# Four DMA transposes per batch queued later, and the last block sums put behind their products, in a fused attention and MLP kernel

## The chip, the cores and the metric

The kernel runs on one core of a Trainium2 chip. The metric is device time in microseconds (us) of one execution. Executions of one kernel agree within about 0.3%. Engines are called PE (TensorE matmul), PEld (TensorE weight load), DVE (VectorE), ACT (ScalarE), POOL (GpSimd) and SP (SyncE, which here only issues DMAs).

## The reference

```python
# u, v: [8, 3008, 256], z: [8, 3008, 64], float32
scores = (z @ z^T) / 3008
attn   = maximum(scores, 0) ** 2
x      = u * (attn @ v)                    # reshaped to [24064, 256]
h      = x @ w_in                          # [24064, 2048]
out    = (h * sigmoid(1.702 * h)) @ w_out  # [24064, 256]
```

The score matrix is symmetric, and the kernel uses that: it computes about half of the blocks and gets the other half by transposing on the DMA engines.

## The kernel before

A batch has 24 blocks of 128 rows in 6 chunks of 512 columns (chunk 5 is short). A *unit* (i, jp) is a pair of row blocks against chunk i: two PE matmuls, a Relu on ScalarE, a square on VectorE into a tile `a`. Where the mirrored block is needed, SyncE issues a DMA transpose of `a` into a tile `tt`. All transposes of a batch go through SyncE's one queue, in program order.

```python
def square(b, i, jp, sc):
    rl = pw.tile([P, 2, CH], F16, name="rl", tag="rl", bufs=3)
    ...
    act.activation(rl, sc, AF.Relu, scale=csc)
    ...                                   # diagonal units: a small transpose into "ad"
    a = pa.tile([P, 2, CH], F16, name="a", tag="a", bufs=21)
    unit[b, i, jp] = a
    dve.tensor_tensor(a, rl, rl, ALU.mult)
    cj = jp // 2
    if cj > i and (b or cj < NCH - 1):
        if (b, i, cj) not in TT:
            TT[b, i, cj] = pa.tile([P, CB, CB, P], F16, name="tt", tag="tt", bufs=14)
        k0 = 2 * (jp % 2)
        sp.dma_start_transpose(
            TT[b, i, cj][:, k0:k0 + 2].rearrange("p r g c -> p (r g) c"),
            a.rearrange("p r c -> p (r c)"),
        )
```

The order of the units puts the last chunk's (10 and 11) ahead of units 6 to 9. Chunk 0 has units 0..5, 10, 11, 6..9, chunk 1 has 2..5, 10, 11, 6..9, and so on:

```python
def pieces(b, i):
    lst = [(i, jp) for jp in range(2 * i if b or i < NCH - 1 else 0, NU)]
    if i == NCH - 1 or b == 0:
        return lst
    k = max(len(lst) - 6, 2)
    return lst[:k] + lst[-2:] + lst[k:-2]
```

Attention of chunk i multiplies the blocks of v with the scores. Each block is used twice (for two halves of the output), and a chunk takes about 11 to 13 us. The blocks j = 20, 21, 22 come last in the first half; for them PE reads the transposes of units (i, 10) and (i, 11), so these are *chunk i's last-chunk tiles*. The transposes of (0, 6) to (0, 9) are read only in the attention of chunks 3 and 4.

Chunk 0's units are computed at the end of the batch before, those of chunks 1 and 2 during attention of chunks 0 and 1.

The MLP's second product is done by a Strassen scheme: seven products P1 to P7 per chunk on PE, with block sums (S1 to S4, two halves each) on VectorE:

```python
prods = products(nst(b))
for q in range(head, nup):
    ...
    up_group(b, q)               # each up group also pops one waiting sum
    product(b, *prods.pop(0))
for kp in prods:                 # only the last batch has any left: 14
    for s_ in SUMS[:2]:
        s_()
    del SUMS[:2]
    product(b, *kp)
```

```python
# in product():
if name in ("P1", "P6", "P7"):
    u_ = ST[b, k, "after" + name] = pw.tile([P, 2, P], F32, name="u" + name, tag="u" + name, bufs=1)
    act.activation(u_, bank, AF.Copy, scale=1.0 / FSC)
...
outs = {"P2": (0, C0, "P2", "P1"), "P7": (1, C1, "P5", "P7"), "P3": (0, C1, "P5", "P6")}
if name in outs:
    o, c, x, u_ = outs[name]
    dve.scalar_tensor_tensor(     # "y"
        y[:, :, o, c], ST[b, k, "bank" + x], 1.0 / FSC, ST[b, k, "after" + u_], ALU.mult, ALU.add,
    )
```

P6, P7 and P4 accumulate onto P1's bank, P3 onto P5's. So a product may have to wait until ScalarE has copied its bank into a `uP` buffer, and each of these buffers exists once: it is free when the `y` of the block before has read it.

## Time and profile before

| | before |
|---|---|
| median time, range (3 runs) | 1206.41 us, 1205.06 to 1208.82 |
| profiled span | 1203.2 us, clock 1.000 |
| PE busy | 1190.2 us |
| PE's waits in all | about 9 us, 6 of them in the start-up |

The page of the kernel before: busy time and share of the span of each engine, TensorE's granted clock in 40 slices, and the chain of waits by engine.

```profile
PE 1190.2 (99%) x11785; PEld 715.2 (59%) x11785; DVE 830.5 (69%) x1277; ACT 770.5 (64%) x903; POOL 307.1 (26%) x363
...
PEclk9999999999999999999999999999999999999999
...
PE 95%; DMA 2%; DVE 2%; ACT 1%; issue 0%; SPq 0%; ACTq 0%; DVEq 0%
```

PE is the limit everywhere. So the change can only win what PE waits. PE's table of waits in the kernel before (engine and line that waited, what for, us in total, times, longest):

```profile
PE o L304 <- DMA tt<-a: 2.0, 5, 0.7
...
PE st L445 <- ACT uP L455: 0.9, 1, 0.9
```

The first line is attention waiting for transposed tiles, the second one product waiting for ScalarE. The change aims at both. Its first target, in SyncE's timeline of batch 2 (start, length, engine, line, operation, count):

```profile
305.06 19.15 SPq L251 DMA_TRANSPOSE tt<-a  x10
324.63 1.19 SPq L238 DMA_TRANSPOSE ad<-a  x1
325.92 11.77 SPq L251 DMA_TRANSPOSE tt<-a  x8
337.80 2.33 SPq L238 DMA_TRANSPOSE ad<-a  x1
```

And PE in the same stretch:

```profile
332.71 0.83 PE L304 MATMUL o<-tt,V 64*128 64x512 f16 x6
334.28 1.04 PE L304 MATMUL o<-tt,V 64*128 64x512 f16 x8 [0.74 <-DMA tt<-a]
```

The group of 10 is chunk 0 (units 2..5, 10, 11, then 6..9); the group of 8 is chunk 1, whose fourth transpose is unit (1, 11). SyncE's queue runs back to back here: an issue takes 1.28 us in the median of all transposes and the next one begins 0.1 us later, so a place in the queue costs about 1.38 us (these 8 took 11.8 us, as the first needed 2.1). PE's matmul at 334.28 us is the first that needs (1, 11). It waited 0.74 us.

The second target is at the kernel's end. These lines of the timeline of the kernel before are VectorE's, ScalarE's and PE's around the wait:

```profile
1186.66 1.95 PE L445 MATMUL st<-WT,s 128*128 128x128 f16 x32
...
1187.40 1.29 DVE L416 TENSOR_TENSOR s<-gt 128x1024 f16<-128x1024 f16 x2
...
1188.61 0.42 DVE L461 SCALAR_TENSOR_TENSOR y<-st,uP 128x256 f32<-128x256 f32 x1
...
1189.12 0.38 ACT L455 ACTIVATE uP<-st 128x256 f32<-128x256 f32 x1 [2.69 <-DVE y L461]
1189.55 1.05 PE L445 MATMUL st<-WT,gt 128*128 128x128 f16 x16 [0.94 <-ACT uP L455]
```

Read upwards: PE's P7 waits for ScalarE's copy, that for VectorE's y, and y stood behind two sums.

### The profile page before, as it was taken

The page shows a single profiled execution, that of the slowest core. Times are in us where ns is not written, and L with a number is a line of the kernel's source. Part 1 is how long each engine was busy: PE and PEld are TensorE (multiplying, and loading weights), DVE is VectorE, ACT ScalarE, POOL GpSimd, SP SyncE. Part 2 cuts the span into 40 slices and gives each one's busy share as a digit, 9 for nine tenths or more (in the row PEclk, how much of TensorE's full clock was granted, in tenths as well). Part 3 has the DMA queues.
Part 4 walks back from the last instruction along what each step waited for, and adds up shares of the span by engine and source line. Part 5 has one row for each costly group of instructions (what it writes and reads, how often), then busy time and mean ns, then how long its engine had stood idle before and what let it go on. Part 6 is the DMA issues. An engine that isn't in the chain of part 4 may idle for free.

```text
span 1203.2 us, 28259 instructions
## 1 busy us (share of the span) xinstructions
PE 1190.2 (99%) x11785; PEld 715.2 (59%) x11785; DVE 830.5 (69%) x1277; ACT 770.5 (64%) x903; POOL 307.1 (26%) x363
## 2 busy tenths in 40 slices
PE   7999999999999999999999999999999999999998
PEld 2446765467644676446765468554775547844577
DVE  7669954597545976469654696648966489564886
ACT  6777684476844768366683666736677376772764
POOL 4144300352004520044200451015510134101000
PEclk9999999999999999999999999999999999999999
DMA  9966399562994639844399454984459754496012
GB/s 225 169 112 129 114 168 158 86 153 72 169 161 89 151 91 174 159 78 137 94 186 146 80 137 98 194 133 76 138 121 183 133 83 149 114 180 117 1 37 71
DMA packets 366592, 152.33 MB, mean 127 GB/s; under 512 B 313312, under 2 KB 358496, under 8 KB 366464
## 3 DMA queue, kind: packets, MB, share of 16 engines
q1 hardware_dynamic: 330320, 114.08, 48.6%
q0 software_dynamic: 35456, 35.86, 14.8%
q8 instruction: 92, 1.51, 0.5%
q10 hardware_dynamic: 688, 0.59, 0.2%
q14 instruction: 36, 0.29, 0.1%
HBM read 60.29 MB, written 24.64 MB: 71 GB/s over the span
## 4 chain that ended last, share of the span: by engine, by line
PE 95%; DMA 2%; DVE 2%; ACT 1%; issue 0%; SPq 0%; ACTq 0%; DVEq 0%
PE o L304 37%; PE hg L345 26%; PE st L445 17%; PE yp L511 8%; PE sc L217 6%; DMA tt<-a 2%; DVE a L245 1%; ACT rl L231 0%; DMA zf<-in_z_dram 0%; DVE gt L354 0%; DVE zst L123 0%; ACT gf L353 0%; DVE s L416 0%; DVE s L418 0%; PE zp L129 0%
## 5 line engine op out<-in xcount | busy, mean ns | idle before, releaser
L353 ACT ACTIVATE gf<-hg 128x1024 f32<-128x1024 f32 (+1 forms) x384 | 385.8, 1007 | 166.0 <-PE hg L345 138.8
L231 ACT ACTIVATE rl<-sc 128x1024 f16<-128x1024 f32 x311 | 308.1, 1025 | 208.0 <-PE sc L217 205.9
L304 PEld LDWEIGHTS <-V 64*128 64x128 f16 (+1 forms) x4052 | 233.9, 94 | 251.4 <-issue 10.0
L345 PE MATMUL hg<-xt,W 128*128 128x512 f16 (+1 forms) x1408 | 354.5, 374 | 0.1
L354 DVE TENSOR_SCALAR gt<-gf 128x1024 f16<-128x1024 f32 (+1 forms) x384 | 275.5, 718 | 89.0 <-ACT gf L353 84.7
L245 DVE TENSOR_TENSOR a<-rl 128x1024 f16<-128x1024 f16 x276 | 192.0, 697 | 183.8 <-ACT rl L231 181.0
L304 PE MATMUL o<-a,V 64*128 64x512 f16 (+2 forms) x2010 | 316.4, 372 | 0.0
L187 POOL DMA_DIRECT2D uq<-in_u_dram x188 | 129.6, 696 | 509.2 <-PE sc L217 343.5
L304 PE MATMUL o<-tt,V 64*128 64x512 f16 (+1 forms) x1762 | 215.3, 376 | 2.0 <-DMA tt<-a 2.0
L345 PEld LDWEIGHTS <-W 128*128 128x128 f16 x1536 | 141.2, 98 | 117.5 <-issue 0.3
L445 PEld LDWEIGHTS <-gt 128*128 128x128 f16 x2176 | 132.5, 98 | 29.8 <-issue 1.1
L217 PE MATMUL sc<-ZT 64*128 64x512 f16 (+1 forms) x692 | 121.3, 366 | 1.9 <-ACT ZT L135 0.9
L445 PEld LDWEIGHTS <-s 128*128 128x128 f16 x1632 | 99.2, 98 | 20.7
L172 POOL CAST V<-vst 128x512 f16<-128x512 f32 x96 | 90.2, 978 | 65.3 <-DMA vst<-in_v_dram 58.3
L511 PE MATMUL yp<-W,gt 64*128 64x256 f16 x1664 | 104.0, 269 | 0.0
L511 PEld LDWEIGHTS <-gt 64*128 64x128 f16 x1664 | 80.7, 94 | 19.0 <-POOLq L84 4.1
L321 DVE TENSOR_TENSOR xt<-o,ut 128x512 f16<-128x512 f32 x80 | 51.5, 685 | 38.1 <-PE o L304 38.1
L445 PE MATMUL st<-WT,gt 128*128 128x128 f16 x1088 | 71.8, 219 | 0.9 <-ACT uP L455 0.9
L445 PE MATMUL st<-W,gt 128*128 128x128 f16 x1088 | 71.7, 219 | 0.0
L445 PE MATMUL st<-WT,s 128*128 128x128 f16 x1088 | 71.5, 219 | 0.0
L455 ACT ACTIVATE uP<-st 128x256 f32<-128x256 f32 x102 | 39.1, 383 | 38.4 <-DVE y L461 33.7
L217 PEld LDWEIGHTS <-ZT 64*128 64x128 f16 x692 | 37.5, 94 | 37.7 <-issue 6.8
(47 smaller groups left out, 627.3 us busy)
## 6 DMA issues: line engine op xcount, KB each, us to landing
vst<-in_v_dram SPq DMA_DIRECT2D x39, 512.0 KB, 5.0
uq<-in_u_dram POOLq DMA_DIRECT2D x156, 128.0 KB, 3.4
out_dram<-y SPq DMA_DIRECT2D x33, 512.0 KB, 3.7
tt<-a SPq DMA_TRANSPOSE x230, 3.6
uq<-in_u_dram POOLq DMA_DIRECT2D x32, 112.0 KB, 2.9
out_dram<-y POOLq DMA_DIRECT2D x7, 512.0 KB, 5.0
vst<-in_v_dram SPq DMA_DIRECT2D x8, 384.0 KB, 4.5
out_dram<-y POOLq DMA_DIRECT2D x7, 384.0 KB, 4.6
```

The source lines that it names most:

```text
L172: pool.tensor_copy(V16[b][:, n0:n0 + VB, k, :].rearrange("p n (q c) -> p n q c", c=QW), vst.rearrange("p n (q k c) -> p n q k c", k=NCC, c ...
L187: eng.dma_start(uq[k * QW:(k + 1) * QW, :n // QW].rearrange("t q k c -> t q (k c)"), src[:, :, cs])
L217: pe.matmul(sc[:, r, :m * P], zt[h, 2 * kp + r, :], zt[h, (qi + 1) * CB - m:(qi + 1) * CB, :], start=True, stop=True,)
L231: act.activation(rl, sc, AF.Relu, scale=csc)
L245: dve.tensor_tensor(a, rl, rl, ALU.mult)
L304: ins = pe.matmul(acc[c][:, :n], V16[b][h, j, c, :], weights(b, i, j)[h], start=(k, m) == first[c], stop=(k, m) == final[c],)
L321: dve.tensor_tensor(x[:, c, :n], acc[c][:, :n], ut[:, :n], ALU.mult)
L345: pe.matmul(hg[:, e, :n], W1[:, c, ff * P:(ff + 1) * P], XT[b, i][:, c, :n], start=(c == 0), stop=(c == NCC - 1),)
L353: act.activation(gf[:, :, :n], hg[:, :, :n], AF.Gelu_apprx_sigmoid, scale=1.0 / FSC)
L354: dve.tensor_scalar(g, gf[:, :, :n], FSC, None, ALU.mult)
L445: pe.matmul(bank[:, m, :], lhs()[:, f, m, :], right[:, ff, :], start=name in ("P1", "P2", "P5") and m == 0 and ff == 0, stop=ff == NFF // ...
L511: ins = pe.matmul(yp[s // per][:, s % per, :], GT[b, k, ff // CB][h, ff % CB, s * P:(s + 1) * P], W2[h, ff, :], start=new, stop=n == last[ ...
```

## The change

Intent: issue transposes in the order in which PE needs them, and let no sum stand on VectorE ahead of the small operation that frees a bank or buffer.

```diff
+    late = []
...
             k0 = 2 * (jp % 2)
-            sp.dma_start_transpose(
-                TT[b, i, cj][:, k0:k0 + 2].rearrange("p r g c -> p (r g) c"),
-                a.rearrange("p r c -> p (r c)"),
-            )
+            def turn_it():
+                sp.dma_start_transpose(
+                    TT[b, i, cj][:, k0:k0 + 2].rearrange("p r g c -> p (r g) c"),
+                    a.rearrange("p r c -> p (r c)"),
+                )
+
+            if b and i == 0 and 6 <= jp < NU - 2:
+                late.append(turn_it)
+                return
+            turn_it()
+            while late and (i, jp) == (1, NU - 1):
+                late.pop(0)()
...
         for kp in prods:
-            for s_ in SUMS[:2]:
-                s_()
-            del SUMS[:2]
             product(b, *kp)
+            if SUMS:
+                SUMS.pop(0)()
```

NU is 12, so the transposes of (0, 6) to (0, 9) now stand behind that of (1, 11). No matmul, transpose or operation of another engine is added or taken away (the traces differ by 28 semaphore instructions of SyncE and VectorE, 28259 against 28231 in all), and PE's order is the same.

## The prediction

> **What bounds the kernel.** TensorE. The busy table gives PE 1190.2 of 1203.2 us; the chain of waits is 95% PE. "Perfetto Trace Analysis" in the Trainium skill (Identifying the Most-Contended Engine) warns that matmul busy time misjudges distance to the roof, as matmuls are pipelined. Here it matters for waits: a 512-column matmul's record lasts 0.376 us, but in the chain ten of them take 1.08, so a record runs about 0.27 us past the moment when the next could start, and a visible gap understates a stall.
>
> PE's waits sum to 9 us, 6 of them in the start-up. The table of waits leaves two targets: attention on transposed tiles (o <- DMA tt), 2.0 us in 5 waits, and the product on ScalarE's copy (st <- uP), 0.94 us once. So the size is fixed: a few us of 1206.
>
> **Part 1, transposes.** Nothing is added or removed; on SyncE's queue four transposes per batch (chunk 0, units 6 to 9), in seven batches, move behind unit 11 of chunk 1, taken in the middle of chunk 0's attention. PE's order is unchanged. The queue issues a transpose per 1.23 to 1.3 us, in order, so four cost 5.2 us. In batch 2's timeline chunk 1's unit 11 was squared by 323.8 us, but its transpose was issued at 330.9 and landed at 334.2; PE wanted it at about 333.4. With four fewer ahead it issues at about 325 and lands near 329. Batches 3, 5 and 7 show the same (restarts at 480.65, 776.03, 1071.24). From the start of the matmuls before (six at 0.108 us) I estimate losses of 0.92, 0.66, 0.34, 0.37: 2.3 us. Batch 6 does not stall there. Batch 1's wait (217.18, 0.4 us) and an invisible one in batch 4 (662.6) are for chunk 3's own late transposes; the change does not touch them.
>
> Price: the moved transposes hold their score tiles longer (estimate: last landing about 480 to 482 in batch 3, reuse by VectorE about 484), so perhaps a short VectorE wait, off PE's path. Chunk 1's units 6 to 9 keep their place in the queue.
>
> **Part 2, sums.** Only the last batch has products left after its last up group (14). There, sums (0.64 us each) stand on VectorE before the y of the product P3 of the block before; that y (1188.61) frees the single uP buffer, so ScalarE copies at 1189.12 and PE's P7 starts at 1189.55 where it could at about 1188.45: 1.1 us lost. After: y follows its product at about 1187.5, the copy ends by 1188.4, P7 starts on time. S2's sums are still done before the last block's P6. The final 3.7 us after PE stay.
>
> **Sum.** 1206.4 - 2.3 - 1.1 = 1203.0 us; I say 1203.2, range 1200.5 to 1206.3, mostly because the runs before spread from 1205.1 to 1208.8. Faster by over 2%: 0.5%; within 2%: 99%; slower: 0.5%.
>
> **What would show it.** Right: PE's waits on tt fall from 2.0 us in 5 to about 0.4 in 1 (batch 1's, near 217 us); st <- uP is gone; PE's busy time nearly unchanged; the profiled span falls from 1203.2 to about 1199.8; in SyncE's queue the tt group ahead of chunk 1's first transpose has 6 instead of 10, the next 12 instead of 8. Wrong on part 1: the waits stay in batches 2, 3, 5, 7, meaning arrival, not queueing, was late. Wrong on part 2: P7 still waits, or the last block's P6 or P7 newly waits on a sum.
>
> **What would make it wrong.** VectorE's waits for score tiles reaching PE; the moved transposes slowing others' landing; noise as large as the gain.

## The result, and the profile after

| | before | after |
|---|---|---|
| median of the 4 runs of the same comparison | 1206.7 us | 1204.2 us |
| range | 1205.06 to 1208.82 | 1202.0 to 1204.53 |
| ratio after/before, 95% interval | | 0.9974, 0.9955 to 0.9994 |
| profiled span | 1203.2 us, clock 1.000 | 1202.2 us, clock 0.998 |

A ratio is the mean time of one kernel's fast runs over that of the other's of the same rounds, so it is not quite the ratio of the medians. The change is clear of noise and within 2%.

The page after, the same lines:

```profile
PE 1192.0 (99%) x11785; PEld 723.3 (60%) x11785; DVE 830.6 (69%) x1277; ACT 770.2 (64%) x903; POOL 308.4 (26%) x363
...
PEclk9999999999999999999999999999999999999999
...
PE 97%; DVE 1%; DMA 1%; ACT 0%; issue 0%; ACTq 0%
```

PE's waits after. The wait for `uP` is gone, and that for transposed tiles has shrunk but not to the 0.4 us in one place that was foreseen:

```profile
PE o L314 <- DMA tt<-a: 1.2, 2, 0.7
```

SyncE in batch 2 after: 6 transposes ahead of chunk 1's first (`ad`), and 12 behind it.

```profile
305.93 11.09 SPq L253 DMA_TRANSPOSE tt<-a  x6
319.40 1.21 SPq L239 DMA_TRANSPOSE ad<-a  x1
321.49 17.07 SPq L253 DMA_TRANSPOSE tt<-a  x12
338.65 1.96 SPq L239 DMA_TRANSPOSE ad<-a  x1
```

PE at the same place after runs through without a wait:

```profile
333.15 0.40 PE L314 MATMUL o<-tt,V 64*128 64x512 f16 x2
333.37 0.40 PE L218 MATMUL sc<-ZT 64*128 64x512 f16 x2
333.59 1.69 PE L314 MATMUL o<-tt,V 64*128 64x512 f16 x14
```

The kernel's end after: y directly behind its product, ScalarE's copy 1.1 us earlier, no wait on PE.

```profile
1186.74 1.95 PE L455 MATMUL st<-WT,s 128*128 128x128 f16 x32
...
1187.48 0.42 DVE L471 SCALAR_TENSOR_TENSOR y<-st,uP 128x256 f32<-128x256 f32 x1
1187.81 1.28 DVE L426 TENSOR_TENSOR s<-gt 128x1024 f16<-128x1024 f16 x2
...
1187.99 0.38 ACT L465 ACTIVATE uP<-st 128x256 f32<-128x256 f32 x1 [1.48 <-DVE y L471]
...
1188.52 1.06 PE L455 MATMUL st<-WT,gt 128*128 128x128 f16 x16
```

PE's 11785 matmuls have the same order in both traces, so they can be laid over each other: take the start of the same matmul in both and see where the difference jumps.

| place (us in the trace before) | jump, after minus before | what |
|---|---|---|
| start-up, up to 19 | +1.45 | clock at half for 3.4 us (+1.68), the rest -0.23; see below |
| 217.2, batch 1, chunk 4 | -0.58 | wait for chunk 4's last-chunk tiles, gone in this run |
| 334.3, batch 2, chunk 1 | -0.91 | the target |
| 480.6, batch 3, chunk 1 | -0.65 | the target |
| 662.6, batch 4, chunk 4 | +0.47 | longer wait for chunk 4's last-chunk tiles |
| 776.0, batch 5, chunk 1 | -0.34 | the target |
| 787.4, batch 5, chunk 2 | +0.89 | **new** wait |
| 936.5, batch 6, chunk 2 | +0.26 | **new** wait |
| 1071.2, batch 7, chunk 1 | -0.37 | the target |
| 1189.6, last P7 | -1.09 | the sums |
| others together | -0.15 | |

The targets give 0.91 + 0.65 + 0.34 + 0.37 + 1.09 = 3.4 us. Of it the profiled run shows only 1.0, for two reasons.

First, the start-up. The stretch from 15 to 20 us of the kernel before, then of the kernel after (columns: busy us and count of PE, PEld, DVE, ACT, POOL, then granted clock, DMA share, GB/s):

```profile
15.00:20.00 5.00, 4.30 (x28) 1.78 (x29) 4.07 (x9) 2.67 (x3) 4.92 (x8) 1.00 1.21 216
```

```profile
15.00:20.00 5.00, 4.54 (x21) 1.85 (x21) 3.30 (x7) 1.94 (x2) 4.73 (x8) 0.68 1.20 208
```

PE did 21 matmuls where it had done 28: the granted clock was half for 3.41 us. The code there is the same in both kernels. Of the 13 full-speed profiles 8 have this stretch, of both orders of transposes, so it is chance and adds noise of about 1.5 us. "TensorE: Matmul & The Clock Gate" in the Trainium skill (Part 1: The HAM clock gate) has the mechanism: the clock falls to one half after an idle window of about 3.4 us that is free-running, so that what falls into it varies from run to run. The length agrees, 3.41 us; the idleness does not, as PE was busy 2.7 of the 5 us before.

Second, the new waits of chunk 2. Call *slack* the time from the landing of chunk i's last-chunk tiles to the PE matmul that reads them first; 0.05 or less (in chunk 0 also the 0.1 of batch 5) means that PE waited for them. From the traces, batches 1 to 7:

| chunk's last-chunk tiles | before | after |
|---|---|---|
| chunk 0 | 2.1 1.8 0.2 3.3 0.1 3.3 1.1 | 2.5 2.4 1.9 3.2 0.3 3.7 1.2 |
| chunk 1 | 0.66 **0.05 0.05** 0.97 **0.04** 0.71 **0.05** | 4.7 3.9 5.4 4.5 5.3 4.6 4.0 |
| chunk 2 | 1.8 0.8 2.5 1.8 2.0 1.9 1.0 | 0.45 0.26 0.64 0.51 **0.04 0.04** 0.62 |
| chunk 3 | 2.0 1.0 2.8 2.3 2.6 2.8 2.1 | 0.7 0.6 1.1 1.1 2.0 0.4 2.0 |
| chunk 4 | **0.05** 0.6 1.5 **0.05 0.05** 0.7 1.8 | 0.7 1.3 0.6 **0.05** 0.7 0.2 1.7 |

Chunk 1 gained 3.5 to 5.3 us of slack, where 1 would have done. Chunk 2 lost most of what it had, and chunk 3 about 1 us. Call *flight* the time from the start of a transpose's issue to its landing. In batch 6 the queue alone made the wait: (2, 11) was issued at 933.56 instead of 931.30 us, 2.26 later, and flew 3.26 us instead of 3.31. In batch 5 the sum is complete: before, slack 2.01 us. After, the transpose of (2, 11) was issued at 782.68 instead of 782.11 (0.57 later), it flew 4.88 us instead of 3.24 (1.63 longer), and PE came 0.65 us earlier, as it no longer waited further up. That is 2.85, so PE was 0.85 us too early. Without the longer flight there would have been no wait. Such a flight came again in turns_only (4.91 us) and not in after_again (3.24); what makes it is not shown. PE and SyncE there, before and then after:

```profile
780.75 8.74 SPq L251 DMA_TRANSPOSE tt<-a  x6
786.71 1.69 PE L304 MATMUL o<-tt,V 64*128 64x512 f16 x14
```

```profile
781.33 9.04 SPq L253 DMA_TRANSPOSE tt<-a  x6
786.07 0.83 PE L314 MATMUL o<-tt,V 64*128 64x512 f16 x6
...
787.60 1.04 PE L314 MATMUL o<-tt,V 64*128 64x512 f16 x8 [0.71 <-DMA tt<-a]
```

Why later at all? In the kernel before, in batch 5, the queue issued without a break from 749 to 796 us. With four transposes taken out of chunk 0's group, SyncE stood still at 759.1 to 760.7 and 761.9 to 762.6 us, as chunk 1's squares were not there yet (its table of waits has a new line, 17.5 us in 7 places, for diagonal transposes waiting on VectorE). All that time the four transposes that had been moved stood ready behind them: VectorE had finished chunk 0's last square at 759.2 us. Then the backlog came back, and part of that lost issue time with it. The change moved work behind a point but did not reduce it.

### The profile page after: what moved, and what is told of

The parts are those of the page before. It is cut to its first block, busy times and chain, and to the rows that moved or that the text cites. A ratio compares the mean times of both kernels' runs of the same rounds, so it can differ in the third digit from the quotient of the medians.

```text
span 1202.2 us, 28231 instructions
## 1 busy us (share of the span) xinstructions
PE 1192.0 (99%) x11785; PEld 723.3 (60%) x11785; DVE 830.6 (69%) x1277; ACT 770.2 (64%) x903; POOL 308.4 (26%) x363
## 4 chain that ended last, share of the span: by engine, by line
PE 97%; DVE 1%; DMA 1%; ACT 0%; issue 0%; ACTq 0%
PE o L314 38%; PE hg L355 27%; PE st L455 18%; PE yp L521 8%; PE sc L218 6%; DMA tt<-a 1%; DVE a L246 0%; PE w L97 0%; DVE gt L364 0%; DVE zst L124 0%; ACT gf L363 0%; DVE s L428 0%; PE zp L130 0%; ACT rl L232 0%; DVE s L426 0%
## 5 line engine op out<-in xcount | busy, mean ns | idle before, releaser
L314 PEld LDWEIGHTS <-V 64*128 64x128 f16 (+1 forms) x4052 | 241.2, 94 | 243.4 <-issue 10.2
```

The source lines that it names most:

```text
L314: ins = pe.matmul(acc[c][:, :n], V16[b][h, j, c, :], weights(b, i, j)[h], start=(k, m) == first[c], stop=(k, m) == final[c],)
```

## Experiments

Theory: PE waits in chunk 1 because four issue slots of SyncE's queue, about 1.3 us each, stand ahead of a transpose whose input has long been ready; and P7 waits because y stands behind sums on VectorE. Rivals: the tiles come late for other reasons (scores late, DMA engines loaded); the gain is in one part alone; it is noise.

All kernels gave correct results. They ran on three chips, each with its own runs of the kernel before: turns_only, sums_only, one_more_ahead and after_again (median before 1207.31 us, 11 runs); chunk1_later_too, all_by_deadline, two_sums_behind and up_two_buffers (1206.98 us, 11 runs); after_third, chunk0_units_early, u4_late and one_sum_ahead (1207.22 us, 9 runs).

### turns_only: the transposes alone

The changed kernel with the old loop of sums put back:

```diff
         for kp in prods:
+            for s_ in SUMS[:2]:
+                s_()
+            del SUMS[:2]
             product(b, *kp)
-            if SUMS:
-                SUMS.pop(0)()
```

> Only the transposes are moved; the sums stay ahead of the products. Theory (queue order): the stalls before the last-chunk matmuls of chunk 1's attention vanish in batches 2, 3, 5, 7 (0.91, 0.65, 0.34, 0.37 us when before and after are laid over each other matmul by matmul, 2.3 us together), PE's wait st <- uP of 0.9 us stays; up to 1.5 us of it is given back as short waits in chunk 2's attention, whose transposes are now issued about 0.6 us later. Net 1 to 2.5 us faster than before. Rival (the gain is all in the sums, or noise of the start-up): the same time as before, and the tt waits of chunk 1 still there.

Measured: 1204.76 us median, ratio 0.9978 (0.9962 to 0.9993). Its jumps against the trace before are -0.93, -0.66, -0.34, -0.37 us at the four targets, and +0.96 and +0.53 in chunk 2 of batches 5 and 6. PE's waits:

```profile
PE o L314 <- DMA tt<-a: 1.4, 3, 0.8
...
PE st L455 <- ACT uP L465: 0.9, 1, 0.9
```

The time falls, which the rival denied, and the wait at the end stays. The give-back in chunk 2 came again, in the same batches and with 0.27 us in batch 1; chunk 3 of batch 7 lost 0.38 us, behind a flight of 4.9 us.

### sums_only: the sums alone

The kernel before with only the second hunk of the change.

> Only the sums are moved. Theory: PE's wait st <- uP is gone, 1.1 us faster than before at the very end, and the five tt waits of about 2.0 us stay. Rival (gain all from the transposes): no change at the end.

Measured: 1206.07 us median, ratio 0.9990 (0.9976 to 1.0005): the timing alone cannot tell it from nothing. The trace can: the jump at the last P7 is -1.09 us and the wait on `uP` is not in the table. The waits for tiles were more than expected in this run, 4.9 us in 6 places, up to 1.7 us; two of them came with flights of 5.4 and 6.6 us in chunks 0 and 4. But they were not the five foreseen: of the four targets only those of batches 3 and 7 waited. In batches 2 and 5 chunk 1 had a slack of 0.32 and 0.42 us, though its transposes had not been moved. So the batches in which chunk 1 waits change from run to run; more on this under after_again.

### one_more_ahead: one more issue slot

The kernel before, with one more transpose in front of chunk 1's, into a spare tile that nothing reads. The tile is small (128x256, the others are 128x1024); what matters is the slot.

```diff
+    spare = const.tile([P, 2, P], F16, name="spare")
...
+            if b and (i, jp) == (0, NU - 3):
+                sp.dma_start_transpose(spare, a[:, 0, :2 * P])
```

> The kernel before with one more small transpose (into a spare tile that nothing reads) in SyncE's queue behind chunk 0's unit 9, once per batch in seven batches. Theory (issue slots of the queue in front of chunk 1's unit 11 are what PE waits for): each extra slot costs about 1.25 us; the stalls in chunk 1's attention grow from 0.92, 0.66, 0.34, 0.37 to about 2.2, 1.9, 1.6, 1.6 in batches 2, 3, 5, 7 and new ones of 0.3 to 0.6 come up in batches 1, 4, 6 (whose slack was 0.66, 0.97, 0.71): about 6 us slower than before. Rival (late arrival of the scores, or the DMA engines' load, sets the landing): under 1 us slower.

Measured: 1214.07 us, ratio 1.0056 (1.0039 to 1.0073), that is 0.0056 x 1207 = 6.8 us slower against the 6 foreseen. SyncE in batch 2:

```profile
307.03 19.53 SPq L252 DMA_TRANSPOSE tt<-a  x10
326.92 1.88 SPq L257 DMA_TRANSPOSE spare<-a  x1
328.90 1.22 SPq L239 DMA_TRANSPOSE ad<-a  x1
330.22 10.89 SPq L252 DMA_TRANSPOSE tt<-a  x8
```

PE's wait on tiles:

```profile
PE o L307 <- DMA tt<-a: 9.1, 7, 2.1
```

The jumps in chunk 1 against the kernel before are +0.84, +1.36, +1.28, +1.60, +0.85, +1.20 us in batches 1, 2, 3, 5, 6, 7 (7.1 in all); batch 4 just escaped with a slack of 0.16 us. The transpose moves a quarter of the bytes of the others, but its place in the queue took 1.33 us in the median, and PE lost 1.2 to 1.6 us more wherever it had waited before. So slots ahead of the queue's critical transpose are what PE pays for. The rival of late scores falls, and so does that of loaded DMA engines: the flight of chunk 1's last tile was 3.2 to 4.2 us here, 3.3 to 4.8 in the kernel before and 3.3 to 4.7 in the changed one.

### after_again and after_third: the changed kernel repeated

> The changed kernel again. Theory: 3 us (0.25%) faster than before in the same rounds; chunk 1's attention without a wait in all seven batches; the waits that are left are in chunks 2 and 4, at places that change from run to run, as they hang on a DMA's flight of 3.2 to 5.7 us. Rival (noise): no difference outside the interval.

Measured: 1204.57 us, ratio 0.9976 (0.9963 to 0.9990). Chunk 1 had a slack of 4.0 to 6.4 us in all batches. Waits for tiles were 2.2 us in 5 places: chunk 2 of batches 4 and 6, chunk 4 of batches 1 and 4, and 1.0 us in chunk 0 of batch 7, where the flight was 5.8 us. Where they fall does change from run to run (chunk 0 had not been expected), but chunk 2 of batch 6 was there each time.

As waits move about, one trace of each kernel is not enough. The experiments give more: five traces have the old order of transposes (before, sums_only, and two_sums_behind, one_sum_ahead and up_two_buffers below), three the changed one (after, turns_only, after_again). What PE lost just before the matmul that reads the last-chunk tiles first, measured against the trace that was quickest at the same place, in us over batches 1 to 7:

| loss in | old order, five traces | changed order, three traces |
|---|---|---|
| chunk 1 | 2.3 1.5 2.2 1.9 3.0 | 0.0 0.0 0.0 |
| chunk 2 | 0.0 0.0 0.0 0.0 0.0 | 1.2 1.8 0.7 |
| chunks 0, 3 and 4 | 1.0 4.4 3.8 0.8 0.3 | 0.7 0.6 2.7 |
| all | 3.3 6.0 6.0 2.7 3.2 | 1.8 2.4 3.4 |

Chunk 1's loss is there in every trace of the old order and in none of the new, and chunk 2's the other way round. The means of the last line differ by 1.7 us; with the 1.1 us of the last P7 that is 2.8, and the three comparisons measured 2.8 to 3.1 us (0.23 to 0.26% of 1207). The part of it that chunks 0, 3 and 4 make, 0.7 us, may be chance.

> The changed kernel a third time, for the same rounds as the two below: ratio to before 0.9975; no wait in chunk 1, two or three short ones in chunks 0, 2 and 4.

Measured: 1204.7 us median of 5, ratio 0.9977 (0.9963 to 0.9990) on four runs. The fifth run, the one with the profile, took 2541.81 us: PE needed about twice its time for everything. It is left out; it returns in the last section. So what was expected of the waits could not be checked. Three comparisons thus gave 0.9974, 0.9976, 0.9977.

### two_sums_behind, one_sum_ahead, up_two_buffers: what in the second part counts

Three looks at the kernel before with part of the second hunk. First the position alone, still two sums per product:

```diff
         for kp in prods:
+            product(b, *kp)
             for s_ in SUMS[:2]:
                 s_()
             del SUMS[:2]
-            product(b, *kp)
```

> The kernel before with each last product put ahead of its two sums, still two per product. Theory (position: y must not stand behind sums on VectorE): the wait of 0.9 us of PE's P7 on ScalarE's copy is gone, as with the whole second part. Rival (thinning from two sums to one per product is what counts): the wait stays, at about half.

Then the thinning alone:

```diff
         for kp in prods:
-            for s_ in SUMS[:2]:
-                s_()
-            del SUMS[:2]
+            if SUMS:
+                SUMS.pop(0)()
             product(b, *kp)
```

> The kernel before with one sum, not two, ahead of each last product: thinned, but not moved behind. Two sums per product behind it moved the 0.8 us wait to the last block's P6; so thinning counts too. Theory (both count): y of P3 now stands behind one sum, about 0.65 us earlier than before, so P7's wait shrinks from 0.9 us to about 0.3 and no wait comes up later. Rival (thinning alone is all of it): no wait at all.

And, with the sums as before, a buffer of its own for the copy that P7 waits for:

```diff
+            if (b, k, name) == (B - 1, 4, "P6"):
+                u_ = ... pw.tile([P, 2, P], F32, name="u" + name, tag="rl", bufs=3)
+            else:
                 u_ = ... pw.tile([P, 2, P], F32, name="u" + name, tag="u" + name, bufs=1)
```

> The kernel before, sums unmoved, but the copy of the last-but-one block's P6 goes to a buffer of its own. Theory (y frees the only uP buffer, ScalarE waits for it, PE waits for ScalarE to free the bank): ScalarE copies at about 1187.8 where it copied at 1189.1, and PE's wait of 0.9 us is gone although y is as late as before. Rival (P7 waits for VectorE itself, its sums or its y): the wait stays.

The wait in each, as PE's timeline or table has it. Position alone:

```profile
1198.05 1.95 PE L445 MATMUL st<-WT,s 128*128 128x128 f16 x32 [0.77 <-ACT uP L455]
```

Thinning alone:

```profile
1189.97 1.05 PE L445 MATMUL st<-WT,gt 128*128 128x128 f16 x16 [0.34 <-ACT uP L455]
```

A buffer of its own (ScalarE's copy, P7 without a wait, then the product that waits now):

```profile
1187.74 0.38 ACT L458 ACTIVATE uP<-st 128x256 f32<-128x256 f32 x1 [1.32 <-PE st L445]
1188.43 1.06 PE L445 MATMUL st<-WT,gt 128*128 128x128 f16 x16
...
1193.00 1.05 PE L445 MATMUL st<-W,s 128*128 128x128 f16 x16 [0.83 <-DVE y L464]
```

With the position alone P7 runs through, but the wait comes up again at the last block's P6, as its copy is behind another y that stands behind two sums. I had expected it gone, so that expectation fell. With thinning alone a third of it stays at P7, as expected. With the buffer P7 runs through too, as the mechanism demands, but P3 of the same block waits 0.83 us for the y that must read its bank first. So the single buffer is only where the delay surfaced. The delay itself is that small y operations stand behind a burst of sums on VectorE; only putting sums behind *and* spreading them removes it. Their times, one run each (1209.03, 1205.40, 1204.96 us), differ by the waits for tiles and the start-up and tell nothing.

### chunk1_later_too: chunk 2 helped in the same way

The changed kernel, with chunk 1's units 6 to 9 (used in chunks 3 and 4) behind (2, 11):

```diff
-            if b and i == 0 and 6 <= jp < NU - 2:
+            if b and i < 2 and 6 <= jp < NU - 2:
                 late.append(turn_it)
                 return
             turn_it()
-            while late and (i, jp) == (1, NU - 1):
+            while late and i in (1, 2) and jp == NU - 1:
                 late.pop(0)()
```

> The changed kernel, with chunk 1's units 6 to 9 (needed only in chunks 3 and 4) moved behind chunk 2's unit 11 in the same way. Theory (queue order): chunk 2's last-chunk tiles, which landed only 0.04 to 0.64 us ahead of PE in the changed kernel and held it in batches 5 and 6, land about 5 us earlier relative to PE; no wait is left in chunks 1 and 2; the waits in chunks 0 and 4 stay as they are. About 1 us faster than the changed kernel, 3.5 us faster than before (ratio 0.997). Rival (the new waits of chunk 2 are a DMA's long flight and not the queue): chunk 2's slack stays under 1 us.

Measured: chunk 2's slack is 6.2 4.8 6.9 5.9 7.4 6.0 6.1 us, so it is the queue's order again. PE's waits after the start-up, from 100 us on:

```profile
PE o L314 <- DMA tt<-a: 0.2, 1, 0.2
```

But the time was 1205.77 us, ratio 0.9984 (0.9970 to 0.9997), no better than the changed kernel's 0.9976. Under 1 us was at stake, and the interval is 3 us wide; the trace shows the waits of this one execution, the timing is undecided.

### all_by_deadline, chunk0_units_early, u4_late: towards a better version

all_by_deadline adds two things to chunk1_later_too: chunk 0's last-chunk units two places earlier, and chunk 4's u loaded earlier.

```diff
-        k = max(len(lst) - 6, 2)
+        k = max(len(lst) - 6, 2) if i else 4
...
-    LOAD = {(3, NJ + 4): 4, (4, NJ + 5): 5}
+    LOAD = {(2, 8): 4, (4, NJ + 5): 5}
```

> As chunk1_later_too, and chunk 0's last-chunk units are computed two places earlier, and chunk 4's u is loaded in chunk 2 and not just ahead of chunk 4's last transposes. Theory: chunk 0's slack (0.13 to 0.33 us in batches 3 and 5) rises by about 3 us; the flight of chunk 4's last transposes (4.4 to 5.9 us) falls towards 3.3 us if the u load beside them is what lengthens it, and with it the waits of chunk 4 in batches 1 and 4. Then PE waits on no transposed tile: 2 us faster than the changed kernel, 4.5 to 5 us faster than before (ratio 0.996). If the u load is not the cause, flights stay at 4.4 to 5.9 us and chunk 4's waits of 0.5 to 1 us stay.

Measured: 1230.36 us, ratio 1.0201 (1.0178 to 1.0224). The expectation was badly wrong. Chunk 0's slack did rise (to 1.5 to 6.0 us) and chunk 4's flights fell to 3.0 to 3.6 us, but chunk 3's tiles came late in every batch: PE lost 0.9 to 3 us each time (1.1 us of it on diagonal tiles). PE's waits, and then three neighbouring stretches of batch 4 (PE busy first, granted clock third from the end):

```profile
PE o L314 <- DMA tt<-a: 12.3, 7, 2.8
```

```profile
650.00:656.00 6.00, 5.35 (x50) 2.50 (x45) 1.98 (x3) 1.02 (x1) 0.00 (x0) 1.00 1.02 171
656.00:659.00 3.00, 0.16 (x4) 0.08 (x4) 0.00 (x0) 0.00 (x0) 0.00 (x0) 0.95 1.01 191
659.00:662.00 3.00, 3.00 (x16) 1.08 (x18) 0.30 (x1) 0.93 (x2) 0.00 (x0) 0.50 0.89 168
```

PE stands for 2.84 us, and then runs at half clock for 3.41, which costs 1.7 us more: this wait is paid about one and a half times. Half clock came at the waits of 2.06, 2.75 and 2.84 us in batches 7, 6 and 4 (in batch 6 for 6.83 us), and at none of the shorter ones, up to 1.54 us here. It need not come: behind a wait of 2.10 us in one_more_ahead (337.61 us) the clock stayed full.

To find which of the two did it, chunk0_units_early leaves the load of u where it was:

> all_by_deadline without its early load of u: chunk 1's units 6 to 9 moved behind chunk 2's unit 11, and chunk 0's last-chunk units two places earlier. If the early u load made the 2% of all_by_deadline (it stretched SyncE's queue in chunk 2: one transpose took 3.5 us to issue there), this is as fast as the changed kernel or up to 1 us faster, chunk 0's slack is 2 us or more and chunk 3's waits are under 0.5 us. If the reordering of chunk 0's units did it, it is 1.5 to 2% slower with chunk 3's waits of 1 to 3 us.

Measured: 1201.92 us, ratio 0.9954 (0.9940 to 0.9967), against 0.9977 (0.9963 to 0.9990) of after_third in the same rounds. So the early load of u was the culprit, as the one difference between the two kernels. It slowed the queue where nothing was to spare: from the issue of (1, 11) to that of (3, 11) all_by_deadline took 28.4 to 30.3 us, this kernel 25.7 to 26.8. The issue of 3.5 us that the expectation names (345.10 us, batch 2) lies within the time of that load, 341.6 to 349.2; but issues of 3.4 us and more are in every full-speed trace (3.45 us at 311.28 in the kernel before, among chunk 0's). How the load slows an issue is not shown. This kernel is the fastest, by more than had been expected: its five runs lie from 1201.19 to 1203.54 us, the changed kernel's four from 1203.08 to 1205.09. The two intervals still touch, so "faster than the changed kernel by about 2.5 us" is likely, not certain. Up to 0.8 us of it may be the start-up: all five runs were granted clock 1.000, which leaves no room for the half clock, against two of the changed kernel's four. Chunk 0's slack is 3.2 to 6.0 us and chunk 3's tiles never held PE. What is left in its profile is chunk 4:

```profile
PE o L314 <- DMA tt<-a: 1.9, 2, 1.7
```

u4_late was to take the load of u away from beside chunk 4's last transposes:

```diff
-    LOAD = {(3, NJ + 4): 4, (4, NJ + 5): 5}
+    LOAD = {(4, 18): 4, (4, NJ + 5): 5}
-    TURN = {..., (4, NJ + 4): 4, (5, 8): 5}
+    TURN = {..., (4, 2 * NJ - 3): 4, (5, 8): 5}
```

> chunk0_units_early with chunk 4's u loaded in the middle of chunk 4's attention instead of just ahead of chunk 4's last transposes, and turned near its end. If the u load lengthens those transposes' flight (4.4 to 5.9 us in the changed kernel, 3.0 to 3.6 where it was loaded early), the flights fall to about 3.3 us, chunk 4's waits in batches 1 and 4 are gone and PE waits on no transposed tile over 0.3 us: about 2 us faster than the changed kernel (ratio to before 0.996). Risk: VectorE waits for u late in chunk 4 and holds PE; then a new wait shows behind chunk 4.

Measured: 1202.71 us, ratio 0.9963 (0.9951 to 0.9976); flights in chunk 4 of 3.5 to 5.7 us, waits in batches 1 and 4 still there, and new ones of 0.2 to 0.5 us in chunk 3 of batches 2, 6 and 7. But the experiment did not do what it was meant to. GpSimd's timeline of the kernel before, then of u4_late:

```profile
207.69 2.61 POOL L187 DMA_DIRECT2D uq<-in_u_dram  x4 [39.19 <-PE sc L217]
```

```profile
207.12 2.60 POOL L188 DMA_DIRECT2D uq<-in_u_dram  x4 [39.19 <-PE sc L218]
```

The load was issued at the same time as ever. It is later in the program, but GpSimd does not follow PE step by step: in each chunk it stops at one empty instruction in the middle (the nop in `post`), and both places come behind the same stop, chunk 3's. So what lengthens those flights stays open. The short flights of all_by_deadline fit the load of u as the cause: during them the mean busy share of the DMA engines was 0.46 to 0.64, against 0.94 to 1.16 in after and after_again. But there PE's long waits in chunk 3 came just before, which can have thinned out other transfers as well.

## Why the prediction was right

- **What bounds it, and the size.** Foreseen 1203.2 us in 1200.5 to 1206.3, measured 1204.2. The bound came from PE's table of waits, and it held. The range was wide enough that the time alone tests little; what tests the prediction are the waits.
- **Part 1.** The four losses were foreseen as 0.92, 0.66, 0.34, 0.37 us and the traces laid over each other give 0.91, 0.65, 0.34, 0.37. Both are read from the same execution of the kernel before, so this shows that its loss was read rightly, not that the loss is always so: in the five traces with the old order it was 1.5 to 3.0 us, in changing batches, and 2.3 lies in the middle by luck. The reading that made this exact was the correction for pipelining: the visible gap was 0.74 us in batch 2, but the loss is counted from the moment the next matmul could have started. "Perfetto Trace Analysis" in the Trainium skill (Identifying the Most-Contended Engine) says that matmul busy time is a bad metric as matmuls are pipelined; here the same overlap hid a fifth of a wait. That queue slots are the cause, one_more_ahead showed.
- **Part 2.** Foreseen 1.1 us, measured 1.09. The reason was half told: the text names the position of y behind the sums, while two_sums_behind shows that position alone only moves the wait. The spreading is needed too.
- **The groups in SyncE's queue** (6 and 12) and PE's wait on `uP` came out as foreseen. VectorE's wait for score tiles, the feared price, did not grow: it was 2.5 us before and 0.8 after in these profiles.
- **What was missed.** "PE's waits on tt fall from 2.0 us in 5 to about 0.4 in 1" was wrong: 1.2 us in 2 other places. The text said that chunk 1's later units "keep their place in the queue" and did not ask what follows them. Chunk 2's tiles were issued 0.5 to 2.7 us later (0.57 in batch 5, to a PE that came earlier), and their slack went from 0.8 to 2.5 us down to 0.04 to 0.64. The give-back is 0.89 + 0.26 us in the profiled run. turns_only, after_again and chunk1_later_too show that the lost slack belongs to the queue; that batch 5 paid 0.89 for it needed a flight of 4.9 us besides.
- **The profiled span** was foreseen as 1199.8 and was 1202.2. The difference is 1.45 us in the start-up, mostly half clock, which is chance, 1.15 of give-back in chunk 2, 0.47 more in chunk 4 of batch 4, less the 0.58 of chunk 4 in batch 1 and 0.15 of small ones.
- **A wrong name.** The waits at 217 and 662 us were put down to chunk 3's transposes in chunk 3's attention; counting matmuls, it is chunk 4. The conclusion, that the change does not touch them, holds.

## What to carry to other kernels

In a queue that issues in order, count slots, not bytes: here one more transpose ahead of the critical one, with a quarter of the bytes, cost its consumer 1.2 to 1.6 us wherever that had no slack. Before moving work behind one deadline, write down the slack of every later deadline in the same queue, because a full queue gives the time back there; and when a change is worth 0.2%, lay the two traces over each other instruction by instruction, as the engine's own order is the same in both, and do it with several traces of each, as the waits fall in other places each time. If a stall vanishes when one buffer is doubled, look whether it comes up at the next: then the delay is in the engine that frees both.

## What the Trainium skill lacked or had wrong

- **"DMA: Bandwidth & Descriptors"** (DMA Transpose (X-bar)) gives constraints but no issue time for a transpose between on-chip tiles of these sizes (the page's one count for on-chip transposes stands in a passage on trn3 and is for 8,192 tiles). Here one issue on SyncE took 1.29 us in the median for 128x1024 fp16 elements, 1.22 us for 128x512 and 1.24 us for 128x256, so it hardly depended on the size; the 128x1024 ones landed 3.1 to 9.7 us after the start of the issue (median 3.6 before, 3.4 after). That any semaphore wait happens on the issuing sequencer before dispatch (same page, Anatomy of one DMA) agrees with SyncE standing still from 759.1 to 760.7 us with four ready transposes behind.
- **"Perfetto Trace Analysis"** warns of matmul busy time for the roof, not for waits (that a matmul's recorded end is modelled stands elsewhere on the page, not what this does to a gap): a visible gap of 0.74 us was a loss of 0.91, and a loss of up to about 0.2 us shows no gap at all.
- **"TensorE: Matmul & The Clock Gate"** (Part 1) agrees in the half clock and its length (3.41 us here). It asks for an idle window of about 3.4 us; here, after the start-up, it came at waits of 2.06, 2.75 and 2.84 us, not at one of 2.10 and at none of up to 1.76, and a start-up stretch in which PE was busy 2.4 to 2.8 of 5 us was followed by it in 8 of 13 profiles.
- **The same page** has a caveat that the records of the clock gate can be unreliable. One execution of the changed kernel took 2541.81 us, PE at about half rate from end to end, and its records gave a granted clock of 1.000. Such an execution must be found by its time, not by its clock.
